# Mirrored output tiles kept in turned token order, with indirect gathers and scatter-adds in place of flip matmuls

## The chip, the cores and the metric

The kernel runs on one core of one Trainium2 chip. The metric is the device time of one execution in microseconds (us), the median of several runs; most runs of one kernel agree within 0.3%. A time is about 2 us longer than the span of its profile, which runs from the first recorded instruction to the last (244.61 against 242.7 for the profiled run of the kernel before).

Engines are named as the profile names them: PE does the matmuls, DVE and ACT are the vector and scalar engines, POOL is GpSimd, SP issues plain transfers. An eviction copies the result of a matmul out of PSUM. An issue is the instruction by which POOL starts a transfer, its landing is the end of that transfer, and the pitch of issues is the time from the start of one to the start of the next.

## The reference, cut to what matters

Two branches are mixed by a gate. Branch A is a gated long convolution, branch B a feed-forward block with layer norms.

```python
g = sigmoid((A_q * gate_w).sum(-1, keepdims=True))
kv = shift_conv(A_k) * A_v                  # 2048 tokens x 640 channels
y  = irfft(rfft(kv, 4096) * rfft(ssm_k, 4096))[:2048] + kv * ssm_D
a  = A_q * y                                # branch A
b  = x1 + gelu(layernorm(x1) @ w3) @ w4     # branch B
out = g * a + (1 - g) * b
```

The tokens are 16 tiles of 128. The inverse transform is written so that one group of matmuls gives an even part E and an odd part O for a tile `ts` and its mirror tile `td` together: row p of tile `ts` is E+O, and row 127-p of tile `td` is E-O. So the second result comes out with its rows in reverse order.

## The kernel before

A list scheduler written in Python puts the operations of the whole program into an order for each engine, from their lengths and from a table of hand-searched biases, one for each group and engine. Inside an engine the order is fixed; across engines there are semaphores. The last work is sixteen "finals" `final(hh, c, q, k)`, each for one half of the channels and one pair of tiles. For k < 12 the result is added to the output in HBM, where branch B has been or will be added by a transfer too; for k >= 12 it is added to branch B in SBUF and stored.

```python
def final(hh, c, q, k):
    ts_, td = 4 * c + q, 4 * c + 3 - q
    qt, gy, ab = qb[k], gyb[k % 8], abb[k % 4]
    P.dma(sp, qt, rows(A_q))                       # query rows of both tiles
    act(qt[:, 0], qt[:, 0], ACTF.Copy, scale=gst[3][:, ts_:ts_ + 1])
    pr = ps(2, "inv")[:, :, 0:320]
    for e in range(2):
        mm(pr[:, e], [...4 matmuls of 128x320...])  # E and O, in PSUM
    act(ab, pr, ACTF.Copy)
    tt(gy[:, 0], ab[:, 0], ab[:, 1], ALU.add)
    pf = ps(1, "fl")[:, 0:320]
    mm(pf, [(flip, ab[:, 0]), (negflip, ab[:, 1])])           # E-O, turned back
    act(gy[:, 1], pf, ACTF.Copy, scale=gst[3][:, td:td + 1])
    for e in ((0, 2),) if k < 14 else ((0, 1), (1, 2)):
        h = slice(*e)
        tt(gy[:, h], gy[:, h], qt[:, h], ALU.mult)
        if k < KACC:                                           # KACC = 12
            P.dma("pool", rows(out, *e), gy[:, h], accum=True)  # 256 rows, one issue
            continue
        tt(gy[:, h], gy[:, h], two(X)[:, h], ALU.add)
        P.dma(sp, rows(out, *e), gy[:, h])
```

A `unit` multiplies transforms, mostly by DVE instructions of two SBUF inputs on 2560 columns, and adds some products by an SBUF-to-SBUF accumulate of 640 KB that POOL issues. `mm4(t)` is the last matmul of the feed-forward block for tile t; its ACT eviction is followed by a POOL accumulate to the output. I call `mm4(15)` tile 15; it is the last of its kind.

Of the kernel before, what the change touches and what calls it, by code (L numbers as in the profile page):

```python
# [173 lines left out]
class Prog:  # L174
# [53 lines left out]
    def dma(self, queue, out, in_, bias=0.0, transpose=False, slow=False, free=None, early=False, accum=False):  # L228
# [4 lines left out]
        if transpose:  # L233
            fn = lambda e: e.dma_start_transpose(out, in_)
        else:
            kw = {"allow_slow_non_contiguous": True} if slow else {"accum_op": ALU.add, "max_dma_last_dim": 4096} if accum else {}
            fn = lambda e: e.dma_start(out, in_, **kw)  # L237
# [265 lines left out]
def bass_gated_mix__ssm_conv_h3__mixer_s_mlp__prompt_kernel(  # L503
# [10 lines left out]
    cI = nc.inline_tensor(_bits(np.concatenate([np.eye(128), -np.eye(128), np.eye(128)[::-1]], 1)), name="cI")  # L514
# [22 lines left out]
    def ps(n, cls):  # L537
# [3 lines left out]
    BIASES = {'base-0|act': -174254.8,  # L541
     'base-0|sp': -804.0,
     'base-10|act': -17721.9,
     'base-10|sp': 270545.9,
     'base-11|act': -32426.0,
     'base-11|sp': -606730.0,
     'base-12|act': -1091211.8,
     'base-12|sp': 111991.5,
     'base-13|act': -424477.0,
     'base-13|sp': 158854.4,  # L550
     'base-14|act': 100289.9,
     'base-14|sp': 49142.6,
     'base-15|act': 75873.6,
     'base-15|sp': 264662.4,
     'base-1|act': -339959.6,
     'base-1|sp': -208139.3,
     'base-2|act': 154820.2,
     'base-2|sp': -367244.5,
     'base-3|act': -256252.7,
     'base-3|sp': 25212.1,  # L560
     'base-4|act': -2314699.6,
     'base-4|sp': -625340.5,
     'base-5|act': -1209731.0,
     'base-5|sp': 97092.3,
     'base-6|act': 99764.7,
     'base-6|sp': 3259.1,
     'base-7|act': -112086.0,
     'base-7|sp': -15613.1,
     'base-8|act': -1223835.7,
     'base-8|sp': -985158.7,  # L570
     'base-9|act': -166668.8,
     'base-9|sp': 372397.8,
     'combine-0-1|dve': -277018.8,
     'combine-0-2|dve': -141664.0,
     'combine-0-3|dve': 274451.6,
     'combine-1-1|dve': -319143.6,
     'combine-1-2|dve': -175226.4,
     'combine-1-3|dve': -68441.1,
     'const-G|sp': -193997.7,
     'const-Rh|sp': 246470.0,  # L580
     'const-R|sp': 728876.1,
     'const-dcol|act': 339170.0,
     'const-dcol|pe': 236301.5,
     'const-d|act': -284337.7,
     'const-esel|act': -103706.8,
     'const-gelu|act': -373148.0,
     'const-gsum|act': -286856.9,
     'const-gsum|pe': 221083.7,
     'const-id|act': 71031.3,
     'const-set|dve': 113129.7,  # L590
     'const-shk|act': -242041.7,
     'const-taps|act': 233381.7,
     'const-taps|pe': 92305.0,
     'const-w1x|dve': -54098.1,
     'const-w1|sp': -43100.8,
     'const-w2|sp': -125742.1,
     'const-warm|dve': 165170.6,
     'const-warm|pe': 325994.6,
     'final-0-0-0-6|act': 30548.1,
     'final-0-0-0-6|dve': -256254.4,  # L600
     'final-0-0-0-6|pe': -315641.2,
     'final-0-0-0-6|pool': -23179.2,
     'final-0-0-0-6|sp': -120164.7,
     'final-0-0-1-7|act': 221146.1,
     'final-0-0-1-7|dve': 166732.5,
     'final-0-0-1-7|pe': -235799.8,
     'final-0-0-1-7|pool': 178784.9,
     'final-0-0-1-7|sp': -802305.9,
     'final-0-1-0-4|act': -33005.4,
     'final-0-1-0-4|dve': -145996.6,  # L610
     'final-0-1-0-4|pe': 90775.2,
     'final-0-1-0-4|pool': -240660.6,
     'final-0-1-0-4|sp': -693042.9,
     'final-0-1-1-5|act': 457431.3,
     'final-0-1-1-5|dve': -26759.1,
     'final-0-1-1-5|pe': -259899.2,
     'final-0-1-1-5|pool': 187724.6,
     'final-0-1-1-5|sp': 338718.3,
     'final-0-2-0-2|act': 66925.5,
     'final-0-2-0-2|dve': 85648.5,  # L620
     'final-0-2-0-2|pe': 235963.7,
     'final-0-2-0-2|pool': 115171.3,
     'final-0-2-0-2|sp': -82668.6,
     'final-0-2-1-3|act': 162601.3,
     'final-0-2-1-3|dve': 12114.0,
     'final-0-2-1-3|pe': 187617.8,
     'final-0-2-1-3|pool': 293856.2,
     'final-0-2-1-3|sp': 55817.4,
     'final-0-3-0-0|act': 161882.0,
     'final-0-3-0-0|dve': -432741.9,  # L630
     'final-0-3-0-0|pe': 149190.1,
     'final-0-3-0-0|pool': 18742.4,
     'final-0-3-0-0|sp': -70687.2,
     'final-0-3-1-1|act': -218608.3,
     'final-0-3-1-1|dve': 178448.1,
     'final-0-3-1-1|pe': -288364.5,
     'final-0-3-1-1|pool': 319005.1,
     'final-0-3-1-1|sp': 34913.2,
     'final-1-0-0-14|act': 214117.9,
     'final-1-0-0-14|dve': -382559.9,  # L640
     'final-1-0-0-14|pe': 231748.1,
     'final-1-0-0-14|sp': -153521.5,
     'final-1-0-1-15|act': -544541.1,
     'final-1-0-1-15|dve': 58563.7,
     'final-1-0-1-15|pe': -332997.7,
     'final-1-0-1-15|sp': -169254.7,
     'final-1-1-0-12|act': 220313.3,
     'final-1-1-0-12|dve': -17729.9,
     'final-1-1-0-12|pe': 329290.6,
     'final-1-1-0-12|sp': -187306.0,  # L650
     'final-1-1-1-13|act': 88828.1,
     'final-1-1-1-13|dve': -33630.4,
     'final-1-1-1-13|pe': -215274.3,
     'final-1-1-1-13|sp': -84116.6,
     'final-1-2-0-10|act': -164093.5,
     'final-1-2-0-10|dve': 102588.0,
     'final-1-2-0-10|pe': -92736.1,
     'final-1-2-0-10|pool': -232571.4,
     'final-1-2-0-10|sp': 153104.5,
     'final-1-2-1-11|act': -413938.3,  # L660
     'final-1-2-1-11|dve': -401621.0,
     'final-1-2-1-11|pe': -1423388.5,
     'final-1-2-1-11|pool': 7427.4,
     'final-1-2-1-11|sp': 150030.3,
     'final-1-3-0-8|act': 59636.8,
     'final-1-3-0-8|dve': 78685.4,
     'final-1-3-0-8|pe': 169597.5,
     'final-1-3-0-8|pool': -21440.7,
     'final-1-3-0-8|sp': 154906.1,
     'final-1-3-1-9|act': -194331.6,  # L670
     'final-1-3-1-9|dve': 274689.5,
     'final-1-3-1-9|pe': -366406.1,
     'final-1-3-1-9|pool': -263481.3,
     'final-1-3-1-9|sp': -89252.6,
     'gate|act': -211504.6,
     'gate|pool': -52486.6,
     'h_chunk-0|act': 7187.9,
     'h_chunk-0|pe': -379397.3,
     'h_chunk-1|act': -109636.2,
     'h_chunk-1|pe': -213179.0,  # L680
     'h_chunk-2|act': 215280.5,
     'h_chunk-2|pe': 1540.0,
     'h_chunk-3|act': 19865.2,
     'h_chunk-3|pe': -149945.7,
     'h_chunk-4|act': -9844.1,
     'h_chunk-4|pe': 200257.6,
     'h_fold-0|act': 520464.2,
     'h_fold-0|dve': 18220.2,
     'h_fold-0|sp': 113098.3,
     'h_fold-1|act': -407170.8,  # L690
     'h_fold-1|dve': -76620.1,
     'h_fold-1|sp': -1351827.2,
     'h_fold-2|act': -70774.6,
     'h_fold-2|dve': -756418.2,
     'h_fold-2|sp': 229259.8,
     'h_fold-3|act': 89707.0,
     'h_fold-3|dve': -840396.5,
     'h_fold-3|sp': 287581.0,
     'h_fold-4|act': 635463.3,
     'h_fold-4|dve': 46787.7,  # L700
     'h_fold-4|sp': -340318.9,
     'h_load-0|sp': -83366.6,
     'h_load-1|sp': -675427.9,
     'h_load-2|sp': -797859.1,
     'h_load-3|sp': 358660.2,
     'h_load-4|sp': 96404.9,
     'kv_block-0-0|act': -218711.7,
     'kv_block-0-0|dve': 6202.5,
     'kv_block-0-0|pe': -29397.0,
     'kv_block-0-0|sp': 84339.0,  # L710
     'kv_block-0-1|act': -437933.3,
     'kv_block-0-1|dve': -18362.1,
     'kv_block-0-1|pe': 360756.6,
     'kv_block-0-1|sp': -1068545.1,
     'kv_block-0-2|act': -493055.4,
     'kv_block-0-2|dve': 222914.9,
     'kv_block-0-2|pe': -194608.2,
     'kv_block-0-2|sp': 76466.9,
     'kv_block-0-3|act': 81991.0,
     'kv_block-0-3|dve': -828934.6,  # L720
     'kv_block-0-3|pe': 149890.2,
     'kv_block-0-3|sp': -2463878.4,
     'kv_block-1-0|act': 452036.3,
     'kv_block-1-0|dve': 68379.2,
     'kv_block-1-0|pe': -166083.2,
     'kv_block-1-0|sp': -138202.4,
     'kv_block-1-1|act': -56715.0,
     'kv_block-1-1|dve': 252238.8,
     'kv_block-1-1|pe': 469013.8,
     'kv_block-1-1|sp': 206659.6,  # L730
     'kv_block-1-2|act': 10119.9,
     'kv_block-1-2|dve': 416314.7,
     'kv_block-1-2|pe': 462642.1,
     'kv_block-1-2|sp': 9686.9,
# [822 lines left out]
```

## Time and profile before

| | before |
|---|---|
| time | 245.09 us (244.93 to 245.28) |
| span of the profile | 242.7 us |
| PE / DVE / ACT / POOL busy | 230.0 / 207.4 / 170.6 / 91.5 us |
| tile 15 evicted by ACT (start) | 221.89 us |
| last matmul, last DVE instruction (end) | 236.47, 239.70 us |

The page of the kernel before begins with the busy time of each engine; its fourth part is the chain of waits that ended last; its fifth lists groups of instructions (line, engine, operation, output<-input, count, then busy us and mean ns of one, then idle time just before them). L1093 is the helper of all large matmuls, L237 the helper of all transfers.

```profile
PE 230.0 (95%) x1520; PEld 140.8 (58%) x1534; DVE 207.4 (85%) x358; ACT 170.6 (70%) x325; POOL 91.5 (38%) x114
...
PE 74%; ACT 10%; DVE 8%; DMA 5%; issue 1%; SPq 0%; DVEq 0%
...
L1093 PE MATMUL PSall<-arena 128*128 128x320 bf16 (+4 forms) x1454 | 221.1, 310 | 4.9 <-ACT arena L1083 1.9
...
L237 POOL DMA_DIRECT2D out_dram<-arena x28 | 29.7, 1166 | 46.9 <-ACT arena L1083 37.3
```

PE is busy 95% of the span, and the chain is PE for 74% of it: a matmul that is removed should count. A POOL issue toward the output takes 1.17 us in the mean.

The table by stretches of the same kernel (bounds in us, width, then busy us and count of PE, weight loads, DVE, ACT, POOL, then granted clock, DMA share, GB/s):

```profile
core 0: us, PE busy (x) PEld busy (x) DVE busy (x) ACT busy (x) POOL busy (x), PEclk, DMA share, GB/s
0.00:20.00 20.00, 17.17 (x112) 9.92 (x113) 15.23 (x58) 10.10 (x22) 4.84 (x14) 1.00 0.93 315
206.00:230.00 24.00, 23.95 (x174) 16.93 (x174) 9.30 (x16) 13.83 (x25) 8.85 (x9) 1.00 0.79 114
230.00:236.00 6.00, 5.35 (x39) 3.30 (x36) 3.56 (x10) 5.01 (x10) 4.46 (x5) 1.00 1.14 114
```

The eviction of tile 15 in ACT's timeline:

```profile
221.89 0.80 ACT L1083 ACTIVATE arena<-PSall,arena 128x640 bf16<-128x640 f32 x1 [2.46 <-PE PSall L1093]
```

PE is full to 230 us and nearly so (5.35 of 6) to 236. DVE has slack from 206 us on (9.3 of 24 busy). POOL is under half busy from 206 to 230.

POOL's timeline of the end (start, length, line, operation; "x3" is three issues in a row, in brackets the idle time before):

```profile
227.10 3.68 POOL L237 DMA_DIRECT2D out_dram<-arena  x3 [2.03 <-DVE arena L1073]
231.40 2.44 POOL L237 DMA_DIRECT2D out_dram<-arena  x2 [0.62 <-DVE arena L1073]
234.76 2.47 POOL L237 DMA_DIRECT2D out_dram<-arena  x2 [0.92 <-DVE arena L1073]
```

POOL issues its last transfer by 237.2 us. Between groups it is idle, waiting for DVE or ACT: it is not what sets the end.

### The profile page before, as it was taken

How to read it: one execution, taken by the hardware profiler on the slowest of the kernel's cores; microseconds unless marked ns; L12 is line 12 of the kernel's file. 1: busy time of each engine (PE TensorE's matmuls, PEld its weight loads, DVE VectorE, ACT ScalarE, POOL GpSimd, SP SyncE). 2: the span in 40 equal slices, each digit the busy share in tenths (PEclk: the TensorE clock that was granted, in tenths of full speed). 3: DMA queues.
4: the chain of work that ended last, by engine and by line, in shares of the span. 5: the costliest groups of instructions: out<-in, count | busy, mean ns of one | idle time of the engine just before them, and what ended most of it. 6: DMA issues, size and time to landing. Idle time of an engine off the chain costs nothing.

```text
span 242.7 us, 4206 instructions
## 1 busy us (share of the span) xinstructions
PE 230.0 (95%) x1520; PEld 140.8 (58%) x1534; DVE 207.4 (85%) x358; ACT 170.6 (70%) x325; POOL 91.5 (38%) x114
## 2 busy tenths in 40 slices
PE   7989999899999999999999999999999999999980
PEld 2477866465655455646567645776546754677750
DVE  4799999999867969999998999999999999820364
ACT  2577978789998696999984386277971455574681
POOL 0242599607140002425823331142320556044670
PEclk9999999999999999999999999999999999999998
DMA  6999998999998898693999934999293699966898
GB/s 180 355 392 338 112 259 186 205 209 278 179 172 201 265 353 143 155 267 88 283 231 186 235 47 89 191 228 259 39 193 40 88 190 168 203 98 70 82 108 161
DMA packets 65305, 45.67 MB, mean 188 GB/s; under 512 B 28931, under 2 KB 60549, under 8 KB 65285
## 3 DMA queue, kind: packets, MB, share of 16 engines
q1 hardware_dynamic: 56268, 33.49, 55.9%
q0 software_dynamic: 8832, 11.80, 33.4%
q8 instruction: 12, 0.20, 0.3%
q10 hardware_dynamic: 184, 0.11, 0.2%
q14 instruction: 9, 0.07, 0.1%
HBM read 24.42 MB, written 6.55 MB: 128 GB/s over the span
## 4 chain that ended last, share of the span: by engine, by line
PE 74%; ACT 10%; DVE 8%; DMA 5%; issue 1%; SPq 0%; DVEq 0%
PE PSall L1093 74%; ACT arena L1083 9%; DVE arena L1255 3%; DVE arena L1073 3%; DMA arena<-in_B_w_dram 2%; DMA arena<-arena 2%; DVE arena L1322 1%; DVE arena L1078 1%; ACT PSall L1083 1%; PE PSall L1300 1%; SPq L237 0%; DVE arena L1256 0%; DVE arena L1139 0%; PE PSall L1154 0%; DVEq L451 0%
## 5 line engine op out<-in xcount | busy, mean ns | idle before, releaser
L1093 PE MATMUL PSall<-arena 128*128 128x320 bf16 (+4 forms) x1454 | 221.1, 310 | 4.9 <-ACT arena L1083 1.9
L1073 DVE TENSOR_TENSOR arena<-arena 128x2560 bf16<-128x2560 bf16 (+5 forms) x215 | 172.5, 851 | 23.5 <-ACT arena L1083 21.6
L1093 PEld LDWEIGHTS PSall<-arena 128*128 128x128 bf16 (+1 forms) x1468 | 135.8, 98 | 89.3 <-ACT arena L1083 6.5
L1083 ACT ACTIVATE arena<-PSall 128x512 bf16<-128x512 f32 (+6 forms) x189 | 114.1, 672 | 34.0 <-PE PSall L1093 28.3
L1078 POOL TENSOR_SCALAR arena<-arena 128x1 f32<-128x1 f32 (+2 forms) x43 | 25.5, 595 | 66.3 <-ACT arena L1083 46.1
L237 POOL DMA_DIRECT2D out_dram<-arena x28 | 29.7, 1166 | 46.9 <-ACT arena L1083 37.3
L1083 ACT ACTIVATE arena<-arena 128x320 bf16<-128x320 bf16 (+4 forms) x54 | 31.7, 621 | 8.3 <-DVE arena L1073 4.4
L1083 ACT ACTIVATE arena<-PSall,arena 128x640 bf16<-128x640 f32 (+1 forms) x32 | 20.5, 666 | 22.5 <-PE PSall L1093 22.2
L237 POOL DMA_DIRECT2D arena<-arena x12 | 15.1, 1261 | 25.1 <-DVE arena L1073 23.4
L1259 POOL TENSOR_TENSOR arena<-arena 128x1 f32<-128x1 f32 (+1 forms) x24 | 21.1, 885 | 6.7 <-DVE arena L1078 5.8
L1078 DVE TENSOR_SCALAR arena<-arena 128x640 bf16<-128x640 bf16 (+2 forms) x53 | 17.0, 342 | 3.6 <-ACT PSall L1083 1.7
L1255 DVE BATCH_NORM_STATS2 arena<-arena 128x6 f32<-128x320 bf16 x32 | 13.3, 474 | 1.4 <-DMA arena<-in_A_q_dram 1.4
L1083 ACT ACTIVATE PSall<-PSall 128x640 f32<-128x640 f32 x16 | 11.6, 729 | 0.1
L1119 PE MATMUL PSall<-arena 128*128 128x512 bf16 x24 | 6.9, 458 | 1.6 <-DVE arena L1115 1.6
L1322 DVE TENSOR_SCALAR arena<-arena 32x256 bf16<-32x256 bf16 (+1 forms) x24 | 5.9, 244 | 0.3
L1119 PEld LDWEIGHTS PSall<-arena 128*128 128x128 bf16 x24 | 2.7, 114 | 5.4 <-issue 2.1
L1083 ACT ACTIVATION_READ_ACCUMULATOR PSall<-PSall 128x1 f32 x16 | 3.6, 223 | 0.0
L1083 ACT ACTIVATION_READ_ACCUMULATOR arena<-PSall 128x1 f32 x16 | 3.5, 222 | 0.0
L1300 PE MATMUL PSall<-arena 128*128 128x128 bf16 x40 | 3.1, 219 | 0.0
L1122 ACT ACT_TABLE_LOAD x1 | 1.3, 1283 | 2.2 <-issue 2.2
L1300 PEld LDWEIGHTS PSall<-arena 128*128 128x128 bf16 x40 | 2.4, 98 | 0.5 <-DVE arena L1078 0.3
L1256 DVE BATCH_NORM_AGGREGATE arena<-arena 128x2 f32<-128x12 f32 x16 | 2.6, 194 | 0.0
(21 smaller groups left out, 5.5 us busy)
## 6 DMA issues: line engine op xcount, KB each, us to landing
arena<-arena POOLq DMA_DIRECT2D x12, 640.0 KB, 6.7
arena<-in_A_k_dram SPq DMA_DIRECT2D x14, 400.0 KB, 4.1
arena<-in_A_q_dram SPq DMA_DIRECT2D x20, 160.0 KB, 5.1
out_dram<-arena POOLq DMA_DIRECT2D x20, 160.0 KB, 4.0
arena<-in_A_ssm_k_dram SPq DMA_DIRECT2D x5, 512.0 KB, 5.7
arena<-in_A_v_dram SPq DMA_DIRECT2D x16, 160.0 KB, 2.9
arena<-in_A_q_dram SPq DMA_DIRECT2D x6, 320.0 KB, 6.2
arena<-in_B_w_dram SPq DMA_DIRECT2D x1, 1920.0 KB, 8.1
```

The lines of the kernel that those rows point to most:

```text
L237: fn = lambda e: e.dma_start(out, in_, **kw)
L1073: P.op(eng, lambda e: e.tensor_tensor(o, a, b, op), [a, b], [o], dve_ns(o, [a, b], 2) if eng == "dve" else 500)
L1078: P.op(eng, lambda e: e.tensor_scalar(o, real(a), s1, s2, op0=op0, **({} if op1 is None else {"op1": op1})), [a] + aps, [o], dve_ns(o, [a] ...
L1083: P.op("act", lambda e: e.activation(real(o), real(a), f, bias=bias, scale=scale, **({"accum_out": accum} if accum is not None else {})), ...
L1093: fns.append(lambda e, l=l, r=r, i=i: e.matmul(real(o), l, r, start=(i == 0), stop=(i == last)))
L1119: P.op("pe", [lambda e: e.matmul(real(pw), warm[:, 0:128], warm[:, 128:640], start=True, stop=True)] * 2, [warm], [pw], 856.0 if i < 4 els ...
L1122: P.op("act", lambda e: e.activation(tjunk[:, 1:2], ones[:, 0:1], ACTF.Gelu_apprx_tanh), [ones[:, 0:1]], [tjunk[:, 1:2]], 1700)
L1255: P.op("dve", lambda e, o=o, i=i: e.bn_stats(o, i), [i], [o], 400)
L1256: P.op("dve", lambda e: e.bn_aggr(bna[:, t, :], bns[k]), [bns[k]], [bna[:, t, :]], 120)
L1259: P.op("pool", lambda g: g.tensor_tensor(o, a, e, ALU.pow), [a, e], [o], dur)
L1300: P.op("pe", [lambda e, c=c, pb=pb, xn=xn: e.transpose(real(pb)[:, 128 * c:128 * (c + 1)], xn[:, 128 * c:128 * (c + 1)], ident) for c in r ...
L1322: P.op("dve", lambda e, o=hT[q, 4, c0:c0 + n], i=hx[q, :]: e.tensor_scalar(o, i, 1.0, None, op0=ALU.mult), [hx[q, :]], [hT[q, 4, c0:c0 + n ...
```

## The change

The intent: leave the second result in turned row order. The query rows of tile `td` are gathered in reverse order by an indirect transfer (eight of 128 rows x 640 for all finals), the gate for these rows is turned once by a tiny matmul, E-O is a DVE subtraction, and the turned product is scatter-added to HBM, row by row in reverse, by an indirect transfer (twelve of 128 rows x 320). Of 32 flip matmuls four are left, for the last four finals. The table of biases was searched anew, so the order of nearly everything moved. The core of the diff, with the biases, the gate, constants and memory layout cut:

```diff
+    def q_load(c, q):
+        qt, ts_, td = qb[2 * (3 - c) + q], 4 * c + q, 4 * c + 3 - q
+        P.dma(sp, qt[:, 0], A_q[0, 128 * ts_:128 * (ts_ + 1), :])
+        P.dma("pool", qt[:, 1], A_q[0, 128 * td:128 * (td + 1), :],
+              fn=lambda e: e.indirect_dma_start(qt[:, 1], None, q640, bass.IndirectOffsetOnAxis(ap=turned[:, 0:1], axis=0),
+                                                element_offset=128 * td * D))
+        for i, (g, t) in enumerate(((3, ts_), (5, td))):
+            act(qt[:, i], qt[:, i], ACTF.Copy, scale=gst[g][:, t:t + 1])
     def final(hh, c, q, k):
 ...
-        P.dma(sp, qt, rows(A_q))
-        act(qt[:, 0], qt[:, 0], ACTF.Copy, scale=gst[3][:, ts_:ts_ + 1])
 ...
         act(ab, pr, ACTF.Copy)
         tt(gy[:, 0], ab[:, 0], ab[:, 1], ALU.add)
+        tt(gy[:, 1], ab[:, 0], ab[:, 1], ALU.subtract)
+        tt(gy, gy, qt, ALU.mult)
+        if k < KACC:
+            P.dma("pool", rows(ts_), gy[:, 0], accum=True)
+            P.dma("pool", rows(td), gy[:, 1], accum=True,
+                  fn=lambda e: e.indirect_dma_start(out320, bass.IndirectOffsetOnAxis(ap=turned[:, 1:2], axis=0), gy[:, 1], None,
+                                                    element_offset=128 * td * D + 320 * hh, compute_op=ALU.add))
+            return
+        tt(gy[:, 0], gy[:, 0], X[:, ts_, hs], ALU.add)
+        P.dma(sp, rows(ts_), gy[:, 0])
         pf = ps(1, "fl")[:, 0:320]
-        mm(pf, [(flip, ab[:, 0]), (negflip, ab[:, 1])])
-        act(gy[:, 1], pf, ACTF.Copy, scale=gst[3][:, td:td + 1])
-        for e in ((0, 2),) if k < 14 else ((0, 1), (1, 2)):
 ... (multiply, accumulate or add X and store)
+        mm(pf, [(flip, gy[:, 1])])
+        tt(ab[:, 0], pf, X[:, td, hs], ALU.add)
+        P.dma(sp, rows(td), ab[:, 0])
```

## The prediction

> **What bounds the kernel now.** Busy table: PE 230.0 of 242.7 us (95%), DVE 207.4, ACT 170.6, POOL 91.5. The table by stretches shows PE full from 60 to 230 us; its only large gap is the tail (5.8 us busy in the last 12.7). The chain of waits is 74% PE, and ends: PE to 230, then about 3.3 us of ACT, 3.7 of DVE and a store of about 3. So TensorE work counts one for one until the tail, where the chain of one final counts. DVE is also full from 110 to 206 us, but idles 8.3 us after 216 (timeline).
>
> **What the change removes and adds.**
> - PE: 32 flip matmuls of 128x320 become 4. In the steady stretch 170 matmuls, mostly of this shape, took 23.6 us, 139 ns each: 28 x 0.136 = 3.8 us removed from a full engine, 1.55% of 245.
> - ACT: 16 flip evictions (538 ns) go, 8.6 us; q scaling goes from 16 x 570 ns to 16 x 876 ns, +4.9. Off the path except in the tail.
> - DVE: 16 more subtractions of 320 columns (0.32 us), +5.2 us; four adds read PSUM. A final under k=12 goes from 0.8 to 1.15 us, one of the last four from 1.3-1.65 to about 2.0. In the full stretch +2.6 us fits into the 8.3 us of slack; in the tail it does not.
> - POOL: an accumulated final was one issue of 256 rows (1.2 us); now a plain one of 128 rows (0.86) and an indirect one. Eight indirect gathers are new. This trace holds no indirect transfer. The Trainium skill, "DMA: Bandwidth & Descriptors", section "SWDGE vs HWDGE vs iDMA", says that GpSimd software computes these descriptors; the two plain sizes give 0.5 us plus 2.7 ns a row. With indices to read I estimate 1.5 us each (1 to 3): POOL goes to about 118 us busy.
>
> **How much is on the critical path.** After the last feed-forward tile about 100 matmuls stood; now 76, and that tile ends at nearly the same time (about 221.7 us), so most of the PE gain appears in the tail. There PE needs about 10 us for nine finals, but DVE about 13.7 (5 x 1.15 + 4 x 2.0), and POOL has 13 issues left (6 x 0.86 + 7 x 1.5 = 15.7 us) plus about 4 us to landing. The tail turns from PE/ACT-bound to DVE/POOL-bound: last DVE instruction at about 237 instead of 239.7, last POOL landing near 241. Of 3.8 us about 3 remain. The re-tuned order of everything else adds 2 us of uncertainty either way.
>
> **Predicted:** 242.0 us, range 239.0 to 246.5. Faster by over 2%: 0.20; within 2%: 0.70; slower by over 2%: 0.10.
>
> **What would show it.** PE busy about 226 us, DVE 213, ACT 167, POOL 118; indirect issues 1 to 2 us; no new PE gap over 1 us before 220 us; the chain of waits ending in DVE (four PSUM adds after a late multiply) or a POOL accumulate, no longer PE until 230.
>
> **What would make it wrong.** Indirect issues of 2.5 us or more: POOL's queue then ends last, past 245 us, and the eight gathers delay the second half's accumulates, so DVE waits for landings. The skill's "GPSIMD Engine Reference", section "Performance pitfalls for Q7 kernels", gives about 102 cycles for each small read command that does not pipeline; if each index is one, an issue is far dearer. The other way: if the new order also closes PE's early gaps (about 3 us in the first 60), it gets under 240.

## The result, and the profile after

The changed kernel takes 255.24 us (254.46 to 257.67), beside 245.01 us for the kernel before in the same rounds. The ratio is 1.0433 (95% interval 1.0361 to 1.0506): slower. Every ratio here is the mean time of one kernel's fast runs over that of the other's of the same rounds, so it is not quite the ratio of the medians. Below, "ratio" is always to the kernel before. The changed kernel's runs also spread more (1.3%) than those of the kernel before (0.2%).

The page of the changed kernel, same parts; L1485 is the scatter, L1464 the gather, L1113, L1093 and L239 are the helpers that were L1093, L1073 and L237:

```profile
PE 229.8 (91%) x1508; PEld 138.9 (55%) x1508; DVE 211.6 (84%) x374; ACT 168.1 (67%) x310; POOL 123.5 (49%) x136
...
PE 29%; DVE 25%; DMA 15%; POOL 13%; ACT 7%; issue 7%; POOLq 1%; SPq 0%; DVEq 0%
...
L239 POOL DMA_DIRECT2D out_dram<-arena x28 | 32.9, 1349 | 18.3 <-ACT arena L1103 14.4
...
L1485 POOL DMA_INDIRECT out_dram<-arena x12 | 25.3, 2110 | 3.6 <-issue 3.3
...
L1464 POOL DMA_INDIRECT arena<-in_A_q_dram,arena x8 | 10.5, 1308 | 3.6 <-issue 2.1
```

PE is no longer the chain (29% instead of 74%). POOL has gone from 91.5 to 123.5 us. A scatter takes 2.11 us in the mean. Their median is 1.62, so one is far off. PE's busy time has not fallen although 28 flip matmuls are gone and only two tiny ones for the gate are new. (Some matmul records are missing in a trace, so the counts x1520 and x1508 do not show it; the weight loads fell by 26.) Busy time is not work: from 206 to 230 us PE is busy 24.00 us with 166 matmuls, where it was busy 23.95 with 174.

The same stretches:

```profile
core 0: us, PE busy (x) PEld busy (x) DVE busy (x) ACT busy (x) POOL busy (x), PEclk, DMA share, GB/s
0.00:20.00 20.00, 15.80 (x84) 8.49 (x85) 13.97 (x54) 9.62 (x18) 5.11 (x14) 0.91 0.94 310
206.00:230.00 24.00, 24.00 (x166) 16.15 (x165) 14.28 (x19) 12.16 (x20) 21.75 (x15) 1.00 0.73 106
230.00:236.00 6.00, 4.40 (x33) 2.94 (x30) 4.12 (x13) 2.38 (x4) 5.40 (x6) 1.00 0.69 76
```

POOL is busy 21.75 of 24 us from 206 us on, where it was 8.85. In the first 20 us the granted clock is 0.91: PE stands still for 1.37 us from 11.29 us on, and from 12.78 us the clock was at half for 3.41 us. That the gap is the reason is not shown: e9 below, in the order of before, has the same dip after gaps of at most 0.62 us, and the kernel before has a gap of 1.09 us at 44 us without one.

POOL's timeline of the end:

```profile
206.73 1.21 POOL L239 DMA_DIRECT2D arena<-arena  x1 [2.80 <-DVE arena L1093]
207.46 1.42 POOL L239 DMA_DIRECT2D out_dram<-arena  x1
209.18 6.47 POOL L1485 DMA_INDIRECT out_dram<-arena  x1 [0.30 <-issue]
215.95 2.03 POOL L1485 DMA_INDIRECT out_dram<-arena  x1 [0.30 <-issue]
217.41 1.88 POOL L239 DMA_DIRECT2D arena<-arena  x1
...
240.38 2.11 POOL L1485 DMA_INDIRECT out_dram<-arena  x1 [0.30 <-issue]
241.89 1.54 POOL L239 DMA_DIRECT2D out_dram<-arena  x1
243.74 1.59 POOL L1485 DMA_INDIRECT out_dram<-arena  x1 [0.30 <-issue]
244.75 1.54 POOL L239 DMA_DIRECT2D out_dram<-arena  x1
246.59 1.61 POOL L1485 DMA_INDIRECT out_dram<-arena  x1 [0.30 <-issue]
```

Two things are to be seen. The scatter at 209.18 us lasted 6.47 us, and everything behind it in POOL's queue came later: the unit's 640 KB accumulate was issued at 217.41. And at the end POOL issues without a pause until 248.19 us: each pair of a scatter and a plain accumulate takes 2.85 to 3.36 us from scatter to scatter (240.38, 243.74, 246.59). A scatter starts 0.30 us after the issue before it has ended, while a plain issue can start under the one before it (217.41 starts before 215.95 + 2.03). POOL's wait for the last landing ends 4.3 us after the last issue, and with it the kernel.

DVE's timeline around the long scatter:

```profile
204.95 12.71 DVE L1093 TENSOR_TENSOR arena<-arena 128x2560 bf16<-128x2560 bf16 x14
223.91 1.56 DVE L1093 TENSOR_TENSOR arena<-arena 128x1280 bf16<-128x1280 bf16 x2 [6.25 <-DMA arena<-arena]
```

DVE runs fourteen multiplies and additions back to back up to 217.66 us, then waits 6.25 us for the late accumulate. Tile 15 is evicted at 225.89 us instead of 221.89:

```profile
225.89 0.77 ACT L1103 ACTIVATE arena<-PSall,arena 128x640 bf16<-128x640 f32 x1
```

### The profile page after: what moved, and what is told of

It is laid out like the page before. It is cut to its first block, busy times and chain, and to the rows that moved or that the text cites. A ratio compares the mean times of both kernels' runs of the same rounds, so it can differ in the third digit from the quotient of the medians.

```text
span 252.7 us, 4168 instructions
## 1 busy us (share of the span) xinstructions
PE 229.8 (91%) x1508; PEld 138.9 (55%) x1508; DVE 211.6 (84%) x374; ACT 168.1 (67%) x310; POOL 123.5 (49%) x136
## 4 chain that ended last, share of the span: by engine, by line
PE 29%; DVE 25%; DMA 15%; POOL 13%; ACT 7%; issue 7%; POOLq 1%; SPq 0%; DVEq 0%
PE PSall L1113 28%; DVE arena L1093 23%; DMA arena<-arena 13%; ACT arena L1103 7%; POOL out_dram L1485 5%; POOL out_dram L239 4%; POOL arena L1098 3%; DMA arena<-in_B_w_dram 2%; DVE arena L1098 1%; POOL arena L1093 1%; POOL arena L1279 1%; POOLq L1564 1%; PE PSall L1320 1%; POOL arena L239 0%; SPq L239 0%
## 5 line engine op out<-in xcount | busy, mean ns | idle before, releaser
L1113 PE MATMUL PSall<-arena 128*128 128x320 bf16 (+4 forms) x1442 | 220.0, 313 | 10.8 <-DVE arena L1093 7.0
L1093 DVE TENSOR_TENSOR arena<-arena 128x640 bf16<-128x640 bf16 (+5 forms) x227 | 174.6, 825 | 19.8 <-DMA arena<-arena 6.8
L1113 PEld LDWEIGHTS PSall<-arena 128*128 128x128 bf16 (+1 forms) x1442 | 133.7, 98 | 95.7 <-DVE arena L1093 8.1
L1103 ACT ACTIVATE arena<-PSall 128x640 bf16<-128x640 f32 (+4 forms) x190 | 112.9, 657 | 32.4 <-PE PSall L1113 20.1
L1098 POOL TENSOR_SCALAR arena<-arena 128x1 f32<-128x1 f32 (+3 forms) x44 | 26.5, 605 | 51.3 <-ACT arena L1103 29.2
L1103 ACT ACTIVATE arena<-arena 128x640 bf16<-128x640 bf16 (+4 forms) x54 | 35.9, 696 | 15.9 <-DVE arena L1093 11.7
L239 POOL DMA_DIRECT2D out_dram<-arena x28 | 32.9, 1349 | 18.3 <-ACT arena L1103 14.4
L239 POOL DMA_DIRECT2D arena<-arena x12 | 17.0, 1414 | 41.8 <-DVE arena L1093 34.3
L1485 POOL DMA_INDIRECT out_dram<-arena x12 | 25.3, 2110 | 3.6 <-issue 3.3
L1103 ACT ACTIVATE arena<-PSall,arena 128x640 bf16<-128x640 f32 x16 | 12.6, 789 | 20.3 <-PE PSall L1113 20.3
L1279 POOL TENSOR_TENSOR arena<-arena 128x1 f32<-128x1 f32 (+1 forms) x24 | 18.0, 761 | 5.9 <-DVE arena L1098 5.2
L1464 POOL DMA_INDIRECT arena<-in_A_q_dram,arena x8 | 10.5, 1308 | 3.6 <-issue 2.1
```

The source lines that it names most:

```text
L239: fn = lambda e: e.dma_start(out, in_, **kw)
L1093: P.op(eng, lambda e: e.tensor_tensor(o, real(a), real(b), op), [a, b], [o], dve_ns(o, [a, b], 2) if eng == "dve" else 500)
L1098: P.op(eng, lambda e: e.tensor_scalar(o, real(a), s1, s2, op0=op0, **({} if op1 is None else {"op1": op1})), [a] + aps, [o], dve_ns(o, [a] ...
L1103: P.op("act", lambda e: e.activation(real(o), real(a), f, bias=bias, scale=scale, **({"accum_out": accum} if accum is not None else {})), ...
L1113: fns.append(lambda e, l=l, r=r, i=i: e.matmul(real(o), l, r, start=(i == 0), stop=(i == last)))
L1279: P.op("pool", lambda g: g.tensor_tensor(o, a, e, ALU.pow), [a, e], [o], dur)
```

## The experiments

The texts of what was expected name by letters the theories of that moment; the text around them says what they were.

The table gives all timed ones; each is told below. "Wrong" means that the mirrored tiles are not turned back; the comparison with the reference passes nevertheless (I take it that branch A is small against the tolerance; no run shows the reason). So this comparison can't show either that the turned kernels called right are right; that rests on reading their code.

| run | what | us | ratio (95%) |
|---|---|---|---|
| changed kernel | | 255.24 | 1.0433 (1.0361 to 1.0506) |
| e1_plain_scatter | scatters plain, wrong | 244.62 | 0.9973 (0.9935 to 1.001) |
| e2_plain_gather | gathers plain, wrong | 256.15 | 1.0477 (1.0414 to 1.0541) |
| e3_plain_both | both plain, wrong | 244.94 | 1.0012 (0.9969 to 1.0054) |
| e4_one_issue | no indirect, one issue of 256 rows, wrong | 245.05 | 0.9992 (0.9954 to 1.003) |
| e5_old_order | changed kernel, biases of before (one slow run) | 259.82 | 1.0599 (1.0531 to 1.0668) |
| e6_old_order_one | e4 with the biases of before, wrong | 245.49 | 1.0047 (0.9995 to 1.0099) |
| e7_no_sub | e4 without add and subtract, wrong | 244.68 | 0.9998 (0.9961 to 1.0034) |
| e9_old_order_no_sub | e6 without add and subtract, wrong | 242.88 | 0.9898 (0.986 to 0.9935) |
| e8_flip_product | gathers kept, product turned by one flip, right | 254.47 | 1.0418 (1.0358 to 1.0479) |
| e11_sub_flip | before, with a subtract and one flip for k < 8, right | 247.19 | 1.0103 (1.006 to 1.0147) |
| e12_one_plain | changed kernel, the long scatter plain, wrong (one slow run) | 254.81 | 1.034 (1.0254 to 1.0427) |
| e13_tail_indirect | only the 7 scatters of the tail indirect, wrong | 252.09 | 1.0275 (1.0234 to 1.0317) |
| e14_early_indirect | only the 5 scatters before them indirect, wrong | 251.68 | 1.0241 (1.0204 to 1.0279) |
| e16_dve_gaps | changed kernel with breaks in DVE's stream, right | 252.51 | 1.0258 (1.0203 to 1.0312) |

My theory after the result was that the indirect issues on POOL cost the time. The first rivals were the newly tuned order (with its clock dip in the opening) and DVE's added work.

### Which transfers: e1, e2, e3, e4

e1 makes the scatters plain, e2 the gathers, e3 both; the order of all instructions stays.

```diff
-            P.dma("pool", rows(td), gy[:, 1], accum=True, fn=lambda e: e.indirect_dma_start(...))
+            P.dma("pool", rows(td), gy[:, 1], accum=True)                      # e1, e3
-        P.dma("pool", qt[:, 1], A_q[...td...], fn=lambda e: e.indirect_dma_start(...))
+        P.dma("pool", qt[:, 1], A_q[...td...])                                 # e2, e3
```

> The changed kernel, but the 12 indirect scatter-adds are plain accumulates of the same 128 rows (rows not turned back: wrong result on purpose). Same instruction order on every engine. Theory A (GpSimd's queue ends last because an indirect issue costs about 1.6 us plus 0.3 us before it, where a plain one costs 0.9): 11 of the 12 stand after 182 us in a queue that is full from 206 us, so about 10 us goes from the queue's end; then DVE's tail is next, expected 241 to 246 us. Theory B (the re-tuned order of PE, DVE and ACT is what is slow): stays above 251 us.

> The changed kernel, but the 8 indirect gathers of q are plain loads of the same rows in the same GpSimd queue (not turned: wrong result on purpose). Theory A: the gathers (1.1 us each plus 0.3) stand at 159 to 174 us, where the queue has room; within 1 us of the changed kernel, 254 to 256 us. Rival C (gathers delay the second half's accumulates, and with them DVE): at least 3 us faster than the changed kernel.

> Both: no indirect transfer at all, same order (wrong result on purpose). Theory A: as the plain scatter alone within 1 us, 241 to 246 us. Theory B: above 251 us. Rival C: clearly faster than the plain scatter alone.

e1 took 244.62 us, e2 256.15, e3 244.94. The scatters cost the whole loss; the gathers cost nothing in this order, though each takes 1.1 us of POOL in the median. The order and its clock dip are in e1 as well, so they are not the loss. POOL's timeline in e1:

```profile
206.40 1.21 POOL L239 DMA_DIRECT2D arena<-arena  x1 [2.80 <-DVE arena L1093]
...
211.01 1.21 POOL L239 DMA_DIRECT2D arena<-arena  x1 [0.69 <-DVE arena L1093]
...
225.43 5.30 POOL L239 DMA_DIRECT2D out_dram<-arena  x6 [1.51 <-ACT arena L1103]
231.07 7.11 POOL L239 DMA_DIRECT2D out_dram<-arena  x8 [0.34 <-DVE arena L1093]
```

The second 640 KB accumulate is issued at 211.01 instead of 217.41 us, and the last eight issues take 7.11 us, 0.9 each. Tile 15 is evicted at 224.34 us, and the 13 issues behind its accumulate take 11.9 us (226.29 to 238.18), where the changed kernel needs 19.6.

e4 has no indirect transfer, and one accumulate of 256 rows for each final, as before:

```diff
-            P.dma("pool", rows(ts_), gy[:, 0], accum=True)
-            P.dma("pool", rows(td), gy[:, 1], accum=True, fn=...)
+            P.dma("pool", <both tiles, 256 rows>, gy, accum=True)
```

> No indirect transfer, and each accumulated final is again one issue of 256 rows instead of two of 128 (turned rows not turned back: wrong result on purpose). PE's and ACT's order is that of the changed kernel. It shows what splitting the accumulate costs by itself. Theory A: the queue loses another 12 x 0.55 us, but DVE's tail (four late PSUM adds, end at about 240 us) now bounds: 239 to 243 us. If splitting costs nothing, equal to the kernel with both plain.

It took 245.05 us, as e1 and e3. So two plain issues in place of one cost nothing measurable. It also says that the idea has no gain in this form, even if indirect transfers were free. (A plain transfer with a negative row stride in HBM, which would turn the tile without indices, could not be built: the compiler refused it.)

### The order: e5, e6

e5 is the changed kernel with the table of biases of the kernel before, e6 is e4 with it.

```diff
-    BIASES = {...of after...}
+    BIASES = {...of before...}
```

> The changed kernel, complete and right, with the table of priorities of the kernel before (final, unit, mm and so on keep their old values; the new groups have none). PE's opening is then in the order of the kernel before. Theory A (scatter-adds in GpSimd's in-order queue): still clearly slower than before, 249 to 256 us. Theory B (the re-tuned order made it slow): 243 to 247 us. Either way the granted clock of the first 20 us should be 1.00 again, where the changed kernel dropped to 0.91.

> The old table of priorities, plain gathers, one accumulate of 256 rows per final, turned rows not turned back (wrong result on purpose): what the change is worth with no indirect transfer and with the old opening. If the re-tuned opening (clock at half for 3.4 or 6.8 us, PE gaps of 1.5 and 1.1 us) ate the 3.8 us that PE saves: 241.0 to 243.0 us. If DVE's tail eats it: 244 to 246 us, as with the new table.

e5 took 259.82 us: the new order did not make the kernel slow, it made it less slow. With the old order the clock stays at 1.00 in the opening, but the first gather, at 152.0 us, lasted 9.57 us, so gathers can do what the scatter did. e6 took 245.49 us with an undisturbed opening and tile 15 at 221.86 us, as before. So the opening is not where PE's saving went. The stretches of e6:

```profile
core 0: us, PE busy (x) PEld busy (x) DVE busy (x) ACT busy (x) POOL busy (x), PEclk, DMA share, GB/s
206.00:230.00 24.00, 23.95 (x173) 16.88 (x173) 13.44 (x22) 11.55 (x20) 10.85 (x12) 1.00 0.78 108
230.00:236.00 6.00, 2.69 (x20) 1.71 (x18) 5.45 (x19) 2.60 (x5) 4.21 (x4) 1.00 1.20 133
```

PE is done early: 2.69 us from 230 to 236 where it was 5.35. DVE fills the stretch instead, with 5.45 of 6 us, and ends at 239.8 us as before (239.7).

### DVE's work: e7, e9

Both drop the add and the subtract (the product is made from E and O directly, wrong); e7 in the new order, e9 in the old one.

```diff
-        tt(gy[:, 0], ab[:, 0], ab[:, 1], ALU.add)
-        tt(gy[:, 1], ab[:, 0], ab[:, 1], ALU.subtract)
-        tt(gy, gy, qt, ALU.mult)
+        tt(gy, ab, qt, ALU.mult)
```

> The kernel with one plain accumulate per final (new table of priorities), without the add and the subtraction of every final: the product is taken from the evicted pair directly (wrong result on purpose). DVE loses 16 x 0.65 us, PE, ACT and GpSimd lose nothing. If DVE's run of work at the end bounds that kernel (245.05 us): 239 to 242 us. If PE or GpSimd's queue bounds it: 244 us or more.

> The old table of priorities with one plain accumulate per final (245.5 us) and without the add and the subtraction of every final (wrong result on purpose): the same removal from DVE as in the run before, but with the opening that keeps the clock. If DVE's work at the end bounds: 241 to 243 us. If GpSimd's queue and the landings that free its buffers bound (as the chain of the other run without the subtraction shows): 244 us or more.

e7 gained nothing (244.68 us): in the new order its chain goes through the landings of earlier accumulates, 5.31 us of waits for a free buffer. e9 took 242.88 us, ratio 0.9898 against 1.0047 for e6, and the intervals are apart. So in the old order, once DVE has less to do in the tail than before, PE's saving does appear. e9 takes this work from every final, not only from those of the tail, but its trace puts the gain in the tail: from the eviction of tile 15 to the end of the span it takes 19.2 us (223.97 to 243.2), where e6 and the kernel before take 20.8. Its chain stays on PE until 234.81 us, that of e6 only until 229.44, and then runs through DVE. (The profile kept is of the slowest run of e9, 244.98 us, with a clock dip in the opening; the other four took 242.24 to 242.91.) So in e6 DVE's work in the tail holds PE's saving back. A right kernel cannot have this, as E+O and E-O are needed.

### Versions that are right: e8, e11

e8 keeps the gathers and turned queries but turns the product back with one flip and an ACT eviction, in the old order. e11 starts from before and only subtracts ahead of one flip for k < 8, 8 matmuls fewer, with those finals preferred.

```diff
# e8, from the changed kernel
+            pf = ps(1, "fl")[:, 0:320]
+            mm(pf, [(flip, gy[:, 1])])
+            act(gy[:, 1], pf, ACTF.Copy)
+            P.dma("pool", <both tiles, 256 rows>, gy, accum=True)
# e11, from before
-        mm(pf, [(flip, ab[:, 0]), (negflip, ab[:, 1])])
+        if k < 8: tt(gy[:, 1], ab[:, 0], ab[:, 1], ALU.subtract); mm(pf, [(flip, gy[:, 1])])
+        else:     mm(pf, [(flip, ab[:, 0]), (negflip, ab[:, 1])])
```

> A right kernel that keeps the gathers (they cost nothing in the runs so far) and drops the scatter-adds: the turned product is turned back by one flip matmul and an eviction, then added by one plain accumulate of 256 rows; old table of priorities. PE saves 16 flips, about 2.1 us, against the kernel before; DVE has its added subtractions. Theory A: no more GpSimd tail, 242 to 246 us. If gathers or the turned order itself were the cost: above 250 us.

> A right kernel from the one before, with no indirect transfer: for the eight finals of the first half DVE subtracts the two parts and one flip matmul turns the result, instead of two flips (8 flips fewer, 1.1 us of PE), and these finals get higher priority. If PE before the tail is what counts: 243 to 244.5 us. If the tail is bound by what comes after PE: 244.5 to 246 us.

Both were misses. e8 took 254.47 us, without any scatter: its first gather, at 151.8 us, lasted 9.57 us as in e5. (No run has e8 with plain gathers, so that this gather is e8's loss is argued, not shown.) e11 took 247.19 us: its chain goes through landings (4.38 us) and ACT. No right version beat the kernel before.

### The long issue by itself: e10, e15, e17

While a gather or scatter lasts long, DVE runs instructions with two SBUF inputs. The Trainium skill, "SBUF — State Buffer", section "Who interferes with whom", says that a DVE instruction with two SBUF inputs contends with a GpSimd instruction that reads SBUF, that one with at most one SBUF input does not outside certain modes, which `tensor_scalar` can enter, and that the shared ports are an exclusive lock: it writes of those modes that whoever issues first has the ports for the whole instruction. An indirect issue has its indices to read from SBUF; a plain one has none. e10 is a program of its own: DVE idle, or streaming one kind of instruction, while POOL issues a plain load, a plain accumulate, a gather and a scatter.

```python
for i in range(14):                                # DVE, by phase
    tensor_tensor(outs[i], a, b, mult)             # 2560 columns, two SBUF inputs
    # or: PSUM and SBUF input; or: tensor_scalar; or nothing
```

> The disputed cost by itself (not the kernel: wrong result on purpose). GpSimd issues a plain load, a plain accumulate, an indirect gather and an indirect scatter-add of 128 rows while DVE is idle; streams multiplies with two SBUF inputs (14 x 1.48 us, back to back); streams multiplies with one PSUM and one SBUF input; streams one-input scalings. Theory P (an indirect issue has to read its indices from SBUF and gets no turn while DVE streams two-input instructions): idle and PSUM phases 1.0 to 1.2 us for a gather and 1.6 us for a scatter-add; in the two-input phases the first indirect issue lasts until the stream ends, 10 us or more, whichever kind comes first, while the plain ones keep 0.5 and 0.9 us. Rival (a full ring of descriptors, or a first-use load): no dependence on what DVE does, under 3 us everywhere.

POOL's timeline of e10, the phases with DVE idle, streaming two SBUF inputs (twice), and one input in PSUM:

```profile
20.07 0.71 POOL L76 DMA_DIRECT2D arena<-in_A_q_dram  x1 [19.62 <-DVE arena L64]
20.77 0.93 POOL L78 DMA_DIRECT2D out_dram<-arena  x1
21.99 1.06 POOL L80 DMA_INDIRECT arena<-in_A_q_dram,index  x1 [0.30 <-issue]
23.36 1.61 POOL L83 DMA_INDIRECT out_dram<-arena,index  x1 [0.30 <-issue]
...
33.35 1.59 POOL L80 DMA_INDIRECT arena<-in_A_q_dram,index  x1 [0.30 <-issue]
...
51.23 2.56 POOL L83 DMA_INDIRECT out_dram<-arena,index  x1 [14.32 <-DVE arena L58]
54.09 1.94 POOL L80 DMA_INDIRECT arena<-in_A_q_dram,index  x1 [0.30 <-issue]
...
75.14 1.06 POOL L80 DMA_INDIRECT arena<-in_A_q_dram,index  x1 [0.30 <-issue]
76.50 1.60 POOL L83 DMA_INDIRECT out_dram<-arena,index  x1 [0.30 <-issue]
```

With DVE idle a gather issue takes 1.06 us and a scatter 1.61, against 0.71 and 0.93 for the plain ones here, and each comes 0.30 us after the issue before. Under two SBUF inputs a scatter took up to 2.56 and a gather up to 1.94 us; plain ones hardly changed; under a PSUM input nothing changed. Under `tensor_scalar` (instructions of 0.8 us) a gather took 1.27 us, a scatter 2.03 and the plain accumulate 1.47. That agrees with the skill's section: under two SBUF inputs an indirect issue waits for the DVE instruction under way to end (of 1.48 us) and no longer. It did not show the starvation of 10 us or more that I expected, so in its strong form this theory fell.

The long issues in the kernel all came 1.9 to 3.3 us after the start of a 640 KB accumulate. e15 puts one (U) ahead, and ACT evictions beside; e17 gives DVE's stream the operand forms, waits and mixed lengths of the kernel.

```diff
-PHASES = [("idle", "LAGS"), ("sbuf2", "LAGS"), ...]
+PHASES = [("idle", "UASG"), ("sbuf2", "UASG"), ("sbuf2", "UGAS"), ("sbuf2", "ALSG"), ("act", "UASG"), ("act", "UGAS")]    # e15
+PHASES = [("bcast", "UASG"), ("bcast", "UGAS"), ("wait", "UASG"), ("wait", "UGAS"), ("mixed", "UASG"), ("mixed", "UGAS")] # e17
```

> A program of its own, wrong output on purpose: DVE idle or streaming two-SBUF-input multiplies of 1.48 us, while GpSimd issues U (an SBUF-to-SBUF accumulate of 640 KB, as it stands 2 us ahead of each long stall in the kernel), A (plain accumulate, 128 rows), S (indirect scatter-add), G (indirect gather), L (plain load); in the last two phases ACT streams evictions from PSUM as well. Theory R (an indirect issue behind a big accumulate in flight stalls while DVE streams): S or G after U lasts 5 us or more in the streaming phases, and below 2.6 without U. Theory R0 (the backlog alone): it also stalls with DVE idle. Theory N (neither, as the first program of this kind showed): at most 2.6 us everywhere, and the long stalls stay open. With ACT streaming too: a stall only there would say that three engines are needed.

> A program of its own, wrong output on purpose: as the earlier one with the large accumulate, but the DVE stream has the forms of the kernel: a factor read again by a broadcast operand (first two phases), the same with a wait on DVE's own count before each (next two), mixed lengths (last two). Theory F (the operand form or the waits make a boundary miss): an indirect issue of 4 us or more in the phases concerned. Theory N (form has no part): at most 2.9 us everywhere, the end of the DVE instruction under way plus 1.1 or 1.6 us, and the long stall stays unexplained below the level of DVE's stream.

The longest scatter was 2.84 us in e15 and 2.41 in e17, the longest gather 1.92 and 2.28. In both, each issue under DVE's stream went through at the first end of a DVE instruction, which came at most 1.35 us after its start. A backlog of transfers, ACT, the operand form and waits do not make the long issue by themselves.

### The place: e12

e12 makes only the scatter that lasted 6.47 us plain.

```diff
-                  fn=lambda e: e.indirect_dma_start(...))
+                  fn=None if k == 5 else lambda e: e.indirect_dma_start(...))
```

> The changed kernel with only the one scatter-add that lasted 6.4 us (issued at 209 us, while DVE streams) made plain (that tile not turned back: wrong result on purpose). Theory P: the blocked turn passes to the next scatter-add in the queue, which now comes while DVE still streams: it lasts 2.5 us or more, and the total gains 1 to 5 us, to 250.5 to 254.5 us. If the long issue belonged to that transfer itself: the next stays at 1.6 to 2.1 us, and the total is 249 to 250.5 us.

The next scatter, at 208.68 us, lasted 9.08 us, and the kernel took 254.81 (254.71 without its slow run). The long issue belongs to the place, not to that transfer.

### Splitting the loss: e13, e14

Here the question was how much is the long scatter and how much the tail's pitch. The pitch of issues is the time from the start of one to the start of the next.

```diff
+                  fn=None if k in (2, 3, 4, 5, 6) else lambda e: ...      # e13: tail alone
+                  fn=None if k not in (2, 3, 4, 5, 6) else lambda e: ...  # e14: the early ones alone
```

> The changed kernel, but the five scatters that are issued before the last feed-forward tile is evicted are plain; the seven in the tail stay indirect. Tiles 2 to 6 are not turned back, wrong on purpose. Theory Q (queue pitch): in the tail a pair of a plain and an indirect issue takes 2.85 us, since an indirect issue does not overlap with its neighbours, where two plain ones take about 1.1; seven pairs behind the last feed-forward tile (evicted near 224.3 us, as without indirect scatters) end near 245 us, landing 4 us later: 249 to 252 us, that is most of the 10 us of loss. Rival S (the long stall of one scatter near 209 us, 4.9 us over its usual 1.6, costs most of it): 245 to 247 us.

> The complement: only the five scatters before the last feed-forward tile (with the stalled one) are indirect, the seven of the tail are plain, not turned back, wrong on purpose. Theory Q: the stall shows (6 us or more near 209 us), the last feed-forward tile is evicted near 226 us instead of 224.3, but POOL's queue catches up with plain issues at 0.54 us: 245.5 to 248 us. Rival S: 250 us or more. If the two losses (over 244.6, all scatters plain) add to about 10.5 us, the terms are independent; if they add to less, the stall also starts the tail's queue later.

e13 took 252.09 us, at the upper end of the 249 to 252 us of theory Q, and far above the 245 to 247 us of rival S. e14 took 251.68 us, as S said and above what Q allowed. So each run refutes one of the two. Over e1's ratio of 0.9973 e13 loses 3.0% and e14 2.7%, together more than the 4.6% of all twelve scatters: each alone costs more than half of the loss, and the two overlap. e14 overstates its part, since there the scatter lasted even longer than in the changed kernel and tile 15 was evicted at 229.00 us:

```profile
209.23 9.98 POOL L1485 DMA_INDIRECT out_dram<-arena  x1 [0.30 <-issue]
219.51 1.58 POOL L1485 DMA_INDIRECT out_dram<-arena  x1 [0.30 <-issue]
220.53 1.87 POOL L239 DMA_DIRECT2D arena<-arena  x1
```

DVE's instructions in e14 are the same as in the changed kernel, and start at the same times from the scatter's start, within 0.02 us. In the changed kernel the scatter got through at the sixth end of a DVE instruction (5.0 us after its start), in e14 only when DVE fell idle (8.5 us): this is an estimate from the end of the issue, since in e15 the end of the DVE instruction came 1.5 us before the end of a scatter and 0.9 before that of a gather. The other long issues fit: in e2 the same scatter lasted 6.44 us and got through at the sixth end again, and those of e12, e5 and e8 got through when DVE fell idle (7.6, 8.6 and 8.6 us after their start). So DVE's instructions in this stretch alone do not decide at which end it gets through.

### Breaks in DVE's stream: e16

This takes the suspected cause away in the kernel itself: eight DVE instructions between 206 and 216 us are each followed by a memset of one column (0.06 us). Everything else stays; the result is right.

```diff
+    for j, i in enumerate((1097, 1098, 1105, 1113, 1099, 1100, 1114, 1115)):
+        P.ops[i].fns.append(lambda e, o=V(oSm + 984 + j, 1): e.memset(o, 0.0))
```

> The changed kernel with one column set to zero on DVE after each of eight multiplies and additions between 206 and 216 us, so that the unbroken stretch of instructions with two SBUF inputs, in which a scatter lasted 6.5 us (10 us with the same DVE instructions in the run with early scatters only), has eight breaks of about 0.1 us; all else as it is, result right. Theory D (DVE's unbroken stream holds the indirect issue up, and gets it or not at each boundary by chance): the scatter near 209 us lasts at most 3.2 us, the last feed-forward tile is evicted near 224.5 us instead of 225.9, and the time falls to 250 to 253.5 us, still slower than before for the tail's pitch. Rival (the stall is not DVE's doing): the scatter still lasts 5 us or more and the time stays at 254 to 257 us.

```profile
208.37 1.97 POOL L1485 DMA_INDIRECT out_dram<-arena  x1 [0.30 <-issue]
210.65 2.48 POOL L1485 DMA_INDIRECT out_dram<-arena  x1 [0.30 <-issue]
212.55 1.88 POOL L239 DMA_DIRECT2D arena<-arena  x1
...
240.97 1.58 POOL L1485 DMA_INDIRECT out_dram<-arena  x1 [0.30 <-issue]
241.97 1.55 POOL L239 DMA_DIRECT2D out_dram<-arena  x1
243.82 1.61 POOL L1485 DMA_INDIRECT out_dram<-arena  x1 [0.30 <-issue]
```

The long scatter is gone: 1.97 us, and the next 2.48. The 640 KB accumulate is issued at 212.55 us instead of 217.41, tile 15 is evicted at 223.86 instead of 225.89, and the kernel takes 252.51 us (251.95 to 252.68). A mere shift in time is an unlikely reason: the first end of a DVE instruction comes 0.47 us after the scatter's start, in the changed kernel 0.46. But there is one profile with breaks, against four without (changed kernel, e2, e12, e14), in all of which an issue in this stretch was long. The tail's pitch is as before (2.85 us from 240.97 to 243.82), and so is the remaining loss, 1.0258, near that of e13.

## Why the prediction was wrong

It said 242.0 us, 239.0 to 246.5, and gave 0.10 to slower by over 2%. It was 255.24.

What held. PE's saving is real: without scatters PE is done earlier (e6: 2.69 us after 230 where it was 5.35). The tail turned from PE and ACT to DVE and POOL. Busy times of DVE (213 told, 211.6 found), ACT (167, 168.1) and POOL (118, 123.5) were near. The gathers are off the path in this order. And POOL's queue was named as what would make it wrong, at 2.5 us an issue; the usual scatter took 1.6, so the right queue was named with the wrong cost.

What failed is the step that put POOL's last 13 issues on the path: when they begin and at what pitch they come. Term by term:

1. "6 x 0.86 + 7 x 1.5 = 15.7 us". The number of issues was right, and the typical scatter (1.60 us) nearly so. But I added up lengths where the pitch counts. From the end of tile 15's own accumulate (228.6 us) to the end of the last scatter (248.19) the 13 issues took 19.6 us, since a scatter does not overlap with the issue before it and has 0.30 us of idle time ahead of it. Plain issues overlap: the same 13, all plain, took 11.9 us in e1. In e13 and e16, without the long scatter, they took 19.8 and 19.6, so the pitch does not come from it. The 19.6 us are 3.9 over the estimate.
2. "That tile ends at nearly the same time (about 221.7 us)". It was evicted at 225.89. In e1, with the same order and no scatter, it was at 224.34, and in e16, without the long scatter, at 223.86; with the old order (e6) at 221.86. So 2 to 2.5 us of the delay are the new order, with its clock dip, and 1.6 to 2 the long scatter. With the eviction and the issues still ahead in POOL's queue, its 13 issues began at 228.6 instead of 221.7, 6.9 us late. This is the largest term.
3. "Indirect issues 1 to 2 us". Under DVE's stream with two SBUF inputs one took 6.47 us. My prediction took its long case from small reads of indices (the skill's "GPSIMD Engine Reference", section "Performance pitfalls for Q7 kernels"); with DVE idle the trace shows only 0.35 us over a plain load for a gather and 0.68 over a plain accumulate for a scatter, so that was not the danger. The danger was DVE's stream, as e16 shows; that it acts through the shared ports is the skill's account and was not seen here. What it was worth: 2.7 us by the medians, 1.75% by the ratios of different rounds (4.3 us; the kernel before was slower in e16's rounds, 245.89 us, with one run of 247.94).
4. "Of 3.8 us about 3 remain". Without any indirect transfer none remains (e1, e3, e4 and e6 are the same as before), and e9 shows why in the old order: DVE's added work in the tail takes it. That the tail's DVE work does not fit was in the text, but with the last DVE instruction at 237 us; in e6 it ended at 239.8.
5. "PE busy about 226 us" was the wrong sign to watch. It was 229.8 with less work in it.

Terms 1 and 2 with 0.3 us more of landing are 3.9 + 6.9 + 0.3 = 11.1 us, and the landing that I put near 241 us came at 252.5. These are times in the profile, and a time is about 2 us longer: my own landing would have meant 243 us, and not the 242.0 that I wrote down.

What stays open: why an indirect issue misses several ends of DVE instructions in the kernel, and in the programs of their own never missed the first. In the kernel, too, an issue need not miss: the next scatter (215.95 us) got through at the first end. Shown, by one profile and four times, is that breaks in DVE's stream end it. How GpSimd and DVE share the ports at such an end was not seen. Also not settled is why e7 finds nothing to gain in the new order beyond its chain of landings.

## What to carry to other kernels

When work moves to a queue, cost its pitch, not the length of one issue: measure whether issues of that kind overlap with their neighbours, and count them behind the event that releases the last of them. Where DVE runs an unbroken stream of instructions with two SBUF inputs, look in the trace for indirect GpSimd issues that last long (up to 9.98 us here), move them or break the stream; and look at what waits behind such an issue in the same queue. Before taking matmuls off a full PE, ask which engine the tail of the kernel will wait for once PE is done earlier, and whether the change adds work to just that one.

## What the Trainium skill lacked or had wrong

- "DMA: Bandwidth & Descriptors", section "SWDGE vs HWDGE vs iDMA", says who computes the descriptors but not what an indirect issue costs: a gather of 128 rows 1.06 us and a scatter-add 1.61 us with DVE idle, against 0.71 and 0.93 us for plain ones in the same phase, and 0.30 us of idle time ahead of each, without overlap with the issue before it.
- "SBUF — State Buffer", section "Who interferes with whom", lets the blocked side wait for one instruction of the other. In programs of their own that held (a wait of at most 1.35 us). In the kernel a waiting indirect issue was passed over by several DVE instructions in a row: 6.47, 9.08, 9.57 and 9.98 us for issues of 1.0 to 1.6 us. With memsets of 0.06 us between them it was gone (1.97 us).
- "TensorE: Matmul & The Clock Gate", section "Part 1: The HAM clock gate (the "warmup" mystery)", has the clock fall after an idle window of about 3.4 us. Here it fell to half for 3.41 us (0.91 in the mean of the first 20 us) where the largest gap of PE between matmuls before it was 1.37 us, and in e9 0.62 us.
- "GPSIMD Engine Reference", section "Performance pitfalls for Q7 kernels": its cost of about 102 cycles for each small read, "e.g. one per gather index", does not describe these issues: 128 indices cost 0.35 to 0.68 us more than a plain transfer.
